# Index 5 of a fused attention and expert kernel takes index 6's order: a fourth group of seven products in place of four dense row blocks

## The chip, the cores and the metric

The kernel runs on one core of a Trainium2 chip. The metric is the time of one execution on the device in microseconds (us); of several executions the median is given. The core has five engines that work side by side and wait for each other through semaphores: TensorE (PE: matmuls; PEld: the loads of their stationary operands), VectorE (DVE), ScalarE (ACT), GpSimd (POOL) and SyncE (SP), which here issues nearly all transfers.

## The reference

Two steps. First, attention in chunks: `q`, `k` and `v` are (8 batches, 8 heads, 576 rows, 64), and each run of 64 rows attends to itself alone.

```python
scores = scale * np.matmul(q_c, k_c.transpose(0, 1, 2, 4, 3))
attn = np.exp(scores - np.max(scores, axis=-1, keepdims=True))
attn = attn / (np.sum(attn, axis=-1, keepdims=True) + 1e-09)
out = np.matmul(attn, v_c)
```

Then the heads are laid side by side, which gives `x` of 4608 tokens by 512, and a two-layer network with an exact Gelu follows:

```python
h = x @ w_in                                    # w_in 512 x 2048
g = 0.5 * h * (1.0 + erf(h * inv_sqrt2))
return (g @ w_out).astype(np.float32)           # w_out 2048 x 512
```

All inputs and the output are float32.

## The kernel before

The tokens are worked in nine tiles of 512 (`NT = 9`, index `t` from 0 to 8): tile `t` under 8 holds the first 512 rows of batch `t`, tile 8 the last 64 rows of all eight batches. All matmuls are in bfloat16 with sums in float32. One index runs in two halves.

First half, `mm1_seven` (from L599): h = Gelu(x w_in), held transposed in 16 row blocks of 128 features by 512 tokens. A row block can be computed dense, by `mm1_slot` (L450 to L457): four matmuls of 512 columns into one PSUM bank, then a Gelu of 128x512 on ScalarE (L457). Or four row blocks at once form a group, by `seven_rows` (L559): the group's 2 x 2 block product is made from seven block products in place of eight, in the manner of Strassen and Winograd. Each product is four matmuls of 256 columns (L574). It needs sums of blocks of x (`x_sums`, L557, on VectorE, once per tile) and of w_in (made once, early). The steps of a group are:

- `p1` to `p7`: the seven products, into three PSUM banks a, b and d; `p5` also copies its bank to a place in SBUF (`kept`, L586), `p3` ends with a Gelu;
- `s11`: ScalarE copies bank a into b (L587), so that p1 serves twice;
- `s12` and `c22+`: VectorE adds `kept` and bank a (L578);
- `c11`, `c12`, `c22`: Gelu of a finished block, on ScalarE (L582).

A step of group 0 stands without a mark, of group 1 with ', of group 2 with '' and of group 3 with '''. A number in an order (12 to 15) is a dense row block. Group g makes the row blocks 4g to 4g + 3.

Second half, `mm2_seven` (from L668): the output as seven products of its own, 16 matmuls of 256 columns each (L730). Two `Y` steps stand for one product. It needs sums of blocks of h (`S1a` to `S4b`, L653 and L666, VectorE), copies of its first results on ScalarE (L690) and additions on VectorE (L695), and then the stores.

Between these steps stands the attention for the tiles behind: `T0` (totals of the softmax of tile t + 1), `R0` to `R3` (their reciprocals spread out), `AV` (attn times v, TensorE), `X0` to `X3` (x), `XS1` to `XS4` (sums of blocks of x), `KC0` to `KC3` (k of tile t + 2 laid out by chunks, ScalarE), `S` (scores of tile t + 2, TensorE, and their Exp), `P0` to `P3` (partial sums of the softmax of tile t + 2, VectorE: L256 and L259), `exp` and `gelu` (a load of ScalarE's function table).

The order of the work on every engine is the order of the program: a manual schedule, in which each engine runs its own instructions in the order in which they were written, and waits where an operand or a buffer isn't ready. For the indices 4 to 8 that order is a list of steps written out by hand (`FOURTH`, `LATER`, `SIXTH`, `SEVENTH`, `LAST`); the table `WHOLE` (L492) says which index takes which list. The table `FURTHER` (L493) gives the groups 2 and 3 of an index their PSUM pools for the banks a, b and d. There are three pools: `MM` with three banks, `TP` with two, `AT` with three. A bank is taken again once its last reader is done. The place for `kept` of the groups 2 and 3 is an old arrival buffer of a load (`kept_home`, from index 4 on).

Indices 6, 7 and 8 have four groups, index 5 three groups and the dense row blocks 12 to 15.

Of the kernel before, what the change touches and what calls it, by code (L numbers as in the profile page):

```python
# [11 lines left out]
def kernel(  # L12
# [15 lines left out]
    B, H, S, D = q.shape  # L28
# [10 lines left out]
    NT = B + 1  # L39
# [176 lines left out]
    AT, TP, MM = (ps_at, "at"), (ps_tp, "tp"), (ps_mm, "mm")  # L216
# [159 lines left out]
    def att_sum_pe(t, g):  # L376

        pT = tiles[t]["pT", g]
        sT = ps_at.tile([P, MT // P, 2], f32, tag="at", name="sT")
        for m in range(MT // P):  # L380
            nc.tensor.matmul(sT[:, m], pT[:].rearrange("p i c -> p (i c)")[:, m * P:(m + 1) * P], ones_r[:],
                             start=True, stop=True)
        rr = work.tile([P, MT // P, 2], f32, tag="rr", name="rr", bufs=2)
        nc.vector.reciprocal(rr[:], sT[:])

        def spread():
            rc_ps = ps_mm.tile([P, MT], f32, tag="mm", name="rc_ps")
            for m in range(MT // P):
                for r in range(2):
                    nc.tensor.matmul(rc_ps[CH * r:CH * (r + 1), m * P:(m + 1) * P],  # L390
                                     rr[:, m, r:r + 1].to_broadcast([P, D]), ident_f[:],
                                     start=True, stop=True, tile_position=(0, CH * r))
            rc = work.tile([P, NB, 32], f32, tag="rc", name="rc", bufs=4)
            nc.scalar.copy(rc[:].rearrange("p n e -> p (n e)"), rc_ps[:])
            tiles[t]["rc", g] = rc
        return spread
# [53 lines left out]
    def mm1_slot(t, f):  # L450
# [3 lines left out]
        for ks in range(KS):  # L454
# [5 lines left out]
    T0 = 3  # L460
    DENSE = (0,)
    TWICE = tuple(range(2, NT))
    FOURTH = ("p1", "s11", 11, "p1'", "p2", "s11'", "c11", "p6", 9, "p5'", "p5", "p6'", 14, "s12'", "s12", "p2'", 13, 10, "p4'",
# [4 lines left out]
    LATER = ("p1", "s11", "p5", "p1'", "p1''", "p2", "p6", "c11", "s11'", "s11''", 13, "s12", 14, "p2''", "c11''", "p6'", "p4",  # L468
# [5 lines left out]
    SIXTH = ("p1", "s11", "p1''", "s11''", "p5", "p5''", "p2", "p6", "s12", "p6''", "p2''", "s12''", "p1'", "c11", "p7", "c11''",  # L474
# [12 lines left out]
    LAST = ("p1", "p1'", "s11", "p5", "p1'''", "s11'", "p2", "p6", "s12", "c11", "p2'", "p5'''", "p5'", "c11'", "s11'''", "p6'",  # L487
# [4 lines left out]
    WHOLE = {T0 + 1: FOURTH, T0 + 2: LATER, NT - 3: SIXTH, NT - 2: SEVENTH, NT - 1: LAST}  # L492
    FURTHER = {T0 + 2: ((MM, AT, AT),), NT - 3: ((MM, MM, MM), (MM, MM, AT)),  # L493
               NT - 2: ((MM, MM, MM), (MM, AT, MM)), NT - 1: ((MM, TP, AT), (MM, TP, MM))}

    HF = FF // 2
# [102 lines left out]
    def mm1_seven(t, hooks):  # L599
# [9 lines left out]
        if t in TWICE:  # L609
            does.update((step + "'", do) for step, do in  # L610
                        seven_rows(t, 1, {"a": TP, "b": TP, "d": AT}, kept[1], more).items())
            if t not in WHOLE:
                fifth = does["p5'"]
                does["p5'"] = lambda: (more.update(d=bank["b"]), fifth())
        for of, pools in enumerate(FURTHER.get(t, ()), 2):
            if kept_more:
# [3 lines left out]
            does.update((step + "'" * of, do) for step, do in seven_rows(t, of, dict(zip("abd", pools)), home, {}).items())  # L620
        if t in WHOLE:
            order = WHOLE[t][:WHOLE[t].index("Y0")]
        elif t == T0:
# [239 lines left out]
    def act_table(func):  # L863
        nc.scalar.activation(act_scratch[:], rest[:, 0:1], func)  # L864

    with tc.manual_schedule():
# [46 lines left out]
        p2 = att_sum_pe(0, 2)  # L913
        p3 = att_sum_pe(0, 3)
# [63 lines left out]
        def whole_hooks(t):  # L978

            n = t + 1  # L980
            acts = {f"S{i}{'ab'[a]}": lambda i=i, a=a: g_sum(t, i, a) for i in (1, 2, 4) for a in range(2)}
            acts["S3"] = lambda: g_sum(t, 3)
            if n < NT:
                acts.update(T0=lambda: quad_totals(n), AV=lambda: quad_av(n, ALONE),
                            exp=lambda: act_table(Act.Exp), gelu=lambda: act_table(Act.Gelu))
                for m in range(G):
                    acts[f"R{m}"] = lambda m=m: quad_rc(n, m // 2, m % 2)
                    acts[f"X{m}"] = lambda m=m: quad_x(n, m // 2, m % 2)
                    acts[f"XS{m + 1}"] = lambda m=m: x_sums(n, (m,))
            if n + 1 < NT:  # L990
                acts["S"] = lambda: quad_S(n + 1, ALONE)
                for m in range(G):
                    acts[f"KC{m}"] = lambda m=m: k_by_chunk(n + 1, AC, (m,))
                    acts[f"P{m}"] = lambda m=m: quad_part(n + 1, m // 2, m % 2)
            e1, e2, slot = {}, {}, 0
            for step in WHOLE[t]:
                if str(step)[0] == "Y":
                    slot += 1
                elif step in acts:
                    if slot:  # L1000
                        e2.setdefault(slot, []).append(acts[step])
                    else:
                        e1[step] = [acts[step]]
            if t + 4 == NT - 1:
                e2.setdefault(11, []).append(lambda: [load_qk(NT - 1, "q"), pool_cast_qk(NT - 1, "q")])
            return e1, e2
# [17 lines left out]
        for t in range(1, NT):  # L1024
# [40 lines left out]
            exp, gelu = lambda: act_table(Act.Exp), lambda: act_table(Act.Gelu)  # L1065
# [5 lines left out]
            if t <= T0:  # L1071
# [24 lines left out]
                else:  # L1096
# [3 lines left out]
                    e2[13] = parts[1]  # L1100
            if t in WHOLE:
                e1, e2 = whole_hooks(t)
# [29 lines left out]
```

## Time and profile before

| what | value |
| --- | --- |
| median of three runs | 268.07 us (267.96 to 268.8) |
| the profiled execution | 269.33 us, span 266.6 us |
| TensorE busy | 257.2 us, 96% of the span |
| VectorE busy | 226.9 us, 85% |
| ScalarE busy | 198.5 us, 74% |
| GpSimd busy | 89.9 us, 34% |
| index 5, from its first matmul to that of index 6 | 160.60 to 187.18 us |
| index 6, likewise | 187.18 to 213.13 us |

The span is the time from the first to the last instruction of the profiled execution; the time of the whole execution also holds what lies around it. Rows of the views name the line, the engine, the operation, and output and inputs by the program's tile names. A row of the timeline begins with start and length in us and puts neighbours of one kind together (x4); its brackets give the idle time before it and what ended it. Matmuls overlap one another, so a single one is listed as longer than the distance to the next. A line can be a helper's: L574 is every product of a group, L578 every addition of `s12` and `c22+`.

### The profile page before, as it was taken

What the parts mean: (1) busy time and instruction counts of PE and PEld (TensorE: products, weight loads), DVE (VectorE), ACT (ScalarE), POOL (GpSimd) and SP (SyncE); (2) the same over time, 40 slices, a digit from 0 to 9 for tenths busy, and PEclk for the clock granted to TensorE, in tenths of its full rate; (3) what the DMA queues carried; (4) which work ended last, traced back from release to release, by engine and by line L of the source; (5) the groups of instructions that cost most, each with busy time, mean ns of one, the idle gap of its engine ahead of it and who ended that gap; (6) DMA issues with size and microseconds to landing.
All of it is one profiled execution on the core that took longest, in us unless ns stands there. A gap on an engine that the chain in (4) does not pass through costs nothing.

```text
span 266.6 us, 7515 instructions
## 1 busy us (share of the span) xinstructions
PE 257.2 (96%) x3023; PEld 202.2 (76%) x3037; DVE 226.9 (85%) x379; ACT 198.5 (74%) x386; POOL 89.9 (34%) x142
## 2 busy tenths in 40 slices
PE   7699999999999999999999999999999999999994
PEld 2478775556886688668876887788888888888883
DVE  6874877999997998988999899897999999947853
ACT  3766758888676967889977987897799789227820
POOL 7869769431177211910710930305100300000000
PEclk9999999999999999999999999999999999999999
DMA  6999998899799899999889929999863320121014
GB/s 203 283 327 401 394 403 212 236 225 281 224 383 268 198 179 312 234 246 318 218 232 309 249 84 170 231 141 164 233 150 88 98 81 2 42 79 42 2 39 118
DMA packets 104739, 53.97 MB, mean 202 GB/s; under 512 B 72960, under 2 KB 101632, under 8 KB 104704
## 3 DMA queue, kind: packets, MB, share of 16 engines
q1 hardware_dynamic: 104400, 53.23, 76.2%
q8 instruction: 23, 0.38, 0.6%
q10 hardware_dynamic: 304, 0.26, 0.3%
q14 instruction: 12, 0.10, 0.1%
HBM read 36.70 MB, written 9.44 MB: 173 GB/s over the span
## 4 chain that ended last, share of the span: by engine, by line
PE 61%; DMA 15%; SPq 13%; ACT 4%; POOL 3%; DVE 2%; issue 1%; POOLq 0%
PE y_ps L730 30%; PE hs_ps L574 21%; DMA arrival<-in_moe_w_out_dram 8%; SPq L128 6%; PE h_ps L455 5%; SPq L194 4%; DMA arrival<-in_k_dram 3%; SPq L116 3%; DMA arrival<-in_v_dram 2%; DMA k_t<-k_nat 2%; PE av_ps L312 1%; ACT k_bd L188 1%; POOL w_out_sb L853 1%; SPq L118 1%; PE s_ps L239 1%
## 5 line engine op out<-in xcount | busy, mean ns | idle before, releaser
L582 ACT ACTIVATE h<-hs_ps 128x512 bf16<-128x512 f32 x66 | 37.7, 602 | 5.1 <-PE hs_ps L574 4.1
L730 PEld LDWEIGHTS <-h 128*128 128x128 bf16 x384 | 37.1, 98 | 4.9 <-issue 0.2
L164 POOL CAST q_nat<-arrival 128x512 bf16<-128x512 f32 x31 | 21.8, 742 | 53.2 <-DMA arrival<-in_q_dram 40.5
L457 ACT ACTIVATE h<-h_ps 128x512 bf16<-128x512 f32 x49 | 29.3, 601 | 11.6 <-PE h_ps L455 7.3
L455 PE MATMUL h_ps<-x,w_in_sb 128*128 128x512 bf16 x131 | 33.3, 379 | 0.5
L214 POOL CAST v_nat<-arrival 128x1024 bf16<-128x1024 f32 x14 | 15.9, 1143 | 44.3 <-DMA arrival<-in_v_dram 44.3
L730 PE MATMUL y_ps<-v_bd,k_bd 128*128 128x256 bf16 x256 | 29.8, 273 | 0.2
L730 PE MATMUL y_ps<-w_out_sb,h 128*128 128x256 bf16 x256 | 29.8, 273 | 0.0
L574 PEld LDWEIGHTS <-w_in_sb 128*128 128x128 bf16 x264 | 25.7, 98 | 4.6 <-issue 0.2
L730 PEld LDWEIGHTS <-k_bd 128*128 128x128 bf16 x256 | 24.8, 98 | 3.7 <-issue 0.5
L164 POOL CAST k_nat<-arrival 128x512 bf16<-128x512 f32 x30 | 20.5, 718 | 15.6 <-DMA arrival<-in_v_dram 12.0
L574 PE MATMUL hs_ps<-x,w_in_sb 128*128 128x256 bf16 x176 | 24.4, 273 | 0.0
L695 DVE TENSOR_TENSOR kept<-y_ps,kept 128x512 f32<-128x512 f32 (+1 forms) x25 | 16.4, 657 | 6.9 <-issue 4.2
L455 PEld LDWEIGHTS <-w_in_sb 128*128 128x128 bf16 x140 | 13.7, 98 | 11.0
L690 ACT COPY kept<-y_ps 128x512 f32<-128x512 f32 (+1 forms) x26 | 14.4, 558 | 9.7 <-PE y_ps L730 9.5
L864 ACT ACT_TABLE_LOAD x16 | 20.5, 1283 | 1.0 <-PEq L1116 0.7
L730 PE MATMUL y_ps<-v_bd,s_sb 128*128 128x256 bf16 x128 | 16.0, 273 | 0.0
L246 ACT ACTIVATE pT<-s_ps 128x512 bf16<-128x512 f32 x28 | 14.4, 599 | 1.5 <-PE s_ps L239 1.4
L730 PE MATMUL y_ps<-w_out_sb,s 128*128 128x256 bf16 x128 | 15.3, 273 | 0.0
L730 PE MATMUL y_ps<-v_bd,h 128*128 128x256 bf16 x128 | 15.3, 272 | 0.0
L574 PEld LDWEIGHTS <-w_in_more 128*128 128x128 bf16 x128 | 12.5, 98 | 3.6 <-issue 0.4
L429 PE MATMUL h_ps<-x,w_in_sb 128*128 128x256 bf16 x128 | 14.3, 273 | 0.0
(146 smaller groups left out, 558.3 us busy)
## 6 DMA issues: line engine op xcount, KB each, us to landing
arrival<-in_v_dram SPq DMA_DIRECT2D x58, 128.0 KB, 4.4
arrival<-in_q_dram SPq DMA_DIRECT2D x7, 1024.0 KB, 6.8
arrival<-in_k_dram SPq DMA_DIRECT2D x6, 1024.0 KB, 8.0
out_dram<-kept SPq DMA_DIRECT2D x21, 256.0 KB, 2.7
arrival<-in_moe_w_out_dram SPq DMA_DIRECT2D x4, 1024.0 KB, 11.6
arrival<-in_moe_w_in_dram SPq DMA_DIRECT2D x6, 512.0 KB, 7.7
out_dram<-y_sb SPq DMA_DIRECT2D x11, 256.0 KB, 3.0
arrival<-in_k_dram SPq DMA_DIRECT2D x8, 256.0 KB, 5.2
```

Of the source, the lines that this page charges most:

```text
L128: nc.sync.dma_start(to, rows.rearrange("h key d -> key h d"))
L164: copy(st[nm][:, g].rearrange("p j r d -> p r j d"), st[nm + "f"][:, 2 * g:2 * g + 2])
L214: copy(st["v"][:, r::2], st["vf"][:, r::2])
L246: nc.scalar.activation(pT[:].rearrange("p u (c j) -> p u c j", j=J), s_ps[g2][c][:].rearrange("p u (j c) -> p u c j", j=J), Act.Exp, scale ...
L455: (nc.tensor.matmul if t else by_halves)(h_ps[:], w_in_sb[:, ks, f * P:(f + 1) * P], tiles[t]["x"][:, ks, :], start=(ks == 0), stop=(ks == ...
L457: nc.scalar.activation(tiles[t]["h"][:, f, :], h_ps[:], Act.Gelu)
L574: nc.tensor.matmul(hs[:, f], left[:, ks, f * P:(f + 1) * P], right[:, ks], start=(fresh and f == 0 and ks == 0), stop=(ks == 1), skip_grou ...
L582: nc.scalar.activation(h[:, n:n + HM, HD * c:HD * (c + 1)], src, Act.Gelu)
L690: nc.scalar.copy(kept[name][:, ms], ps[:])
L695: nc.vector.tensor_tensor(y_sb[:, ms], ps[:], y_sb[:, ms], op=ADD)
L730: nc.tensor.matmul(to, left(f, m), right[:, f], start=(fresh and (split or m == 0) and f == 0), stop=(f == HF - 1), skip_group_check=True)
L864: nc.scalar.activation(act_scratch[:], rest[:, 0:1], func)
```

## The change

Index 5 drops its own list `LATER` and takes `SIXTH`, the list of index 6. In `SIXTH` the row blocks 12 to 15 are made by group 3 and not one by one. The table of pools changes with it: index 5's group 2 had (MM, AT, AT) and there was no group 3; now group 2 has (MM, MM, MM) and group 3 (MM, MM, AT), as in index 6.

```diff
-    LATER = ("p1", "s11", "p5", "p1'", "p1''", "p2", "p6", "c11", "s11'", "s11''", 13, "s12", 14, "p2''", "c11''", "p6'", "p4",
-             "T0", "c12", "p7", "p5'", "p2'", "p5''", "s12'", "c11'", "c22+", "p6''", 15, "s12''", "p7'", "c22", "c22+'", "p4'",
-             "c12'", "p3", "c22'", "p7''", "R2", "p3'", "c22+''", 12, "p4''", "c22''", "c12''", "p3''", "R3", "S3", "KC2", "S1b",
-             "S1a", "Y0", "Y0", "S2b", "S2a", "AV", "Y1", "KC0", "R1", "X3", "Y1", "X0", "Y2", "X2", "KC3", "exp", "X1", "Y2",
-             "KC1", "Y3", "Y3", "S4a", "Y4", "S4b", "XS1", "S", "XS3", "XS2", "Y4", "P0", "Y5", "gelu", "XS4", "P2", "Y5", "P1",
-             "Y6", "P3", "Y6")
     SIXTH = ("p1", "s11", "p1''", "s11''", "p5", "p5''", "p2", "p6", "s12", "p6''", "p2''", "s12''", "p1'", "c11", "p7", "c11''",
              "s11'", "p5'", "p4''", "p1'''", "p4", "c12''", "p6'", "c12", "T0", "s12'", "s11'''", "p2'", "p7''", "c11'", "p5'''",
              "p6'''", "p2'''", "p7'", "c22+", "c22", "c11'''", "c22+''", "c22''", "p4'", "c12'", "s12'''", "p3", "p7'''", "c22+'",
              "R1", "c22+'''", "p3'", "c22'", "R2", "S1a", "p4'''", "c12'''", "S3", "c22'''", "S1b", "p3''", "p3'''", "Y0", "KC0",
              "AV", "S2a", "Y0", "KC3", "KC2", "Y1", "S2b", "X2", "S4a", "X1", "X0", "R3", "X3", "KC1", "Y1", "Y2", "Y2", "S4b",
              "Y3", "XS1", "XS3", "exp", "Y3", "Y4", "S", "XS2", "Y4", "Y5", "P0", "gelu", "Y5", "Y6", "XS4", "P3", "P1", "P2",
              "Y6")
...
-    WHOLE = {T0 + 1: FOURTH, T0 + 2: LATER, NT - 3: SIXTH, NT - 2: SEVENTH, NT - 1: LAST}
-    FURTHER = {T0 + 2: ((MM, AT, AT),), NT - 3: ((MM, MM, MM), (MM, MM, AT)),
+    WHOLE = {T0 + 1: FOURTH, T0 + 2: SIXTH, NT - 3: SIXTH, NT - 2: SEVENTH, NT - 1: LAST}
+    FURTHER = {T0 + 2: ((MM, MM, MM), (MM, MM, AT)), NT - 3: ((MM, MM, MM), (MM, MM, AT)),
                NT - 2: ((MM, MM, MM), (MM, AT, MM)), NT - 1: ((MM, TP, AT), (MM, TP, MM))}
```

`T0` is 3 here and `NT` 9, so `T0 + 2` is index 5 and `NT - 3` index 6. The lists of the other indices stay, index 8's four groups among them. The unchanged list `SIXTH` is shown because it is what index 5 now runs. Line numbers after the removed list are smaller by six in the changed kernel.

## Prediction

> **What bounds the kernel now.** I read the page first: its busy row and its clock row.
>
> ```profile
> span 266.6 us, 7515 instructions
> PE 257.2 (96%) x3023; PEld 202.2 (76%) x3037; DVE 226.9 (85%) x379; ACT 198.5 (74%) x386; POOL 89.9 (34%) x142
> PEclk9999999999999999999999999999999999999999
> ```
>
> TensorE is busy for 96% of the span and the granted clock never falls. A share for the whole span says little about indices 5 and 6, so I next read the chain of work that ended last there, where the change lies.
>
> ```profile
> 160.76 2.62 PE hs_ps L574 x24
> 163.43 1.67 PE h_ps L455 x7
> ...
> 173.38 1.75 PE y_ps L730 x16
> 175.13 0.66 PE av_ps L312 x64
> ...
> 183.57 3.77 PE y_ps L730 x33
> 187.35 12.23 PE hs_ps L574 x112
> 199.57 0.87 PE y_ps L730 x8
> ```
>
> The chain is nothing but TensorE: no wait on VectorE, ScalarE or a transfer stands in either index. A TensorE instruction that is removed here shortens the span, as long as nobody is late for the one behind it. The third view is the table of windows, cut at the first matmul of each half (first half: tokens times w_in; second: the output products).
>
> ```profile
> 160.60:173.22 12.62, 12.52 (x100) 9.78 (x100) 11.65 (x24) 10.76 (x21) 2.29 (x4) 1.00 1.17 201
> 187.18:199.41 12.23, 12.23 (x114) 10.96 (x112) 11.96 (x25) 11.00 (x22) 1.04 (x1) 1.00 0.82 205
> 173.22:187.18 13.96, 13.91 (x242) 11.93 (x240) 12.20 (x22) 11.97 (x18) 3.52 (x5) 1.00 0.99 147
> 199.41:213.13 13.72, 13.72 (x243) 11.97 (x240) 13.48 (x22) 12.43 (x20) 2.30 (x2) 1.00 0.36 93
> ```
>
> Columns: window, its length, then busy time and count of PE, weight loads, DVE, ACT, POOL, the granted clock, the transfer engines' share, GB/s. The rows are index 5 first half, index 6 first half, index 5 second half, index 6 second half. Index 6 already runs the order that index 5 is to get, so its rows show what that order costs: 12.23 us against 12.62, with TensorE never idle but VectorE busy for 11.96 of 12.23. VectorE is the engine to watch.
>
> **The change part by part.** *The products.* Four dense blocks (4 x 4 matmuls of 512 columns) go, seven products (7 x 4 matmuls of 256) come.
>
> ```profile
> 168.44 1.03 PE L455 MATMUL h_ps<-x,w_in_sb 128*128 128x512 bf16 x4
> 169.30 0.60 PE L574 MATMUL hs_ps<-k_bd,w_in_more 128*128 128x256 bf16 x4
> 169.74 0.60 PE L574 MATMUL hs_ps<-x,w_in_more 128*128 128x256 bf16 x4
> ```
>
> Matmuls overlap, so their spacing counts and not their length: four dense ones take 169.30 - 168.44 = 0.86 us and four of a product 169.74 - 169.30 = 0.44. Out go 4 x 0.86 = 3.45 us, in come 7 x 0.437 = 3.06 (0.437 because index 6's 28 products take 12.23). Saved: 0.39 us, and the windows agree with 12.62 - 12.23 = 0.39. I take -0.39.
>
> TensorE: Matmul & The Clock Gate in the Trainium skill (Back-to-back issue gap) speaks against this exchange: it gives sustained spacings of about 81 ns at 128 columns and 131 at 512. An estimate between the two, some 98 ns at 256, would make the products 28 x 98 = 2.7 us against 16 x 131 = 2.1, a loss of 0.6 us. The rows above show 215 and 109 ns in this very stage, so the trace disagrees with that rule and agrees with the isolated gaps on the same page, which grow with the columns.
>
> *The work on ScalarE and VectorE.* The dense blocks had four evictions through Gelu, the group has four of the same size. New are two copies on ScalarE (s11''', p5''') and two additions on VectorE (s12''', c22+''').
>
> ```profile
> L587 ACT COPY hs_ps<-hs_ps 128x512 f32<-128x512 f32 x4 | 2.3, 582 | 0.0
> L578 DVE TENSOR_TENSOR hs_ps<-hs_ps,arrival 128x512 f32<-128x512 f32 x2 | 1.4, 690 | 0.0
> ```
>
> That is about 2 x 0.58 = 1.2 us more for ScalarE and 2 x 0.69 = 1.4 for VectorE (less where they overlap their neighbours). ScalarE goes from 10.76 to about 12 of 12.2 at the most, index 6 shows 11.00: covered. VectorE goes to what index 6 has, 11.96 of 12.23: covered only if it starts index 5 no later than it starts index 6. So I compared the starts.
>
> ```profile
> 163.26 0.69 DVE L259 TENSOR_REDUCE part<-pt 128x16 f32<-128x512 bf16 x1
> 163.86 0.69 DVE L578 TENSOR_TENSOR hs_ps<-hs_ps,kept_p 128x512 f32<-128x512 f32 x1
> ...
> 190.07 0.70 DVE L578 TENSOR_TENSOR hs_ps<-hs_ps,kept_p 128x512 f32<-128x512 f32 x1
> 190.68 0.69 DVE L578 TENSOR_TENSOR hs_ps<-hs_ps,arrival 128x512 f32<-128x512 f32 x1
> ...
> 196.59 0.68 DVE L578 TENSOR_TENSOR kept_p<-hs_ps,kept_p 128x512 f32<-128x512 f32 x1
> ...
> 197.87 0.69 DVE L578 TENSOR_TENSOR arrival<-hs_ps,arrival 128x512 f32<-128x512 f32 x1
> ```
>
> s12 starts 163.86 - 160.60 = 3.26 us into index 5 and 190.07 - 187.18 = 2.89 into index 6, both times straight behind the partial sums (L259) that the stage before left over. Index 5 is 0.37 us worse off, and that is unchanged by the edit. In the new order s12 is wanted early: p7 is the tenth product, and it adds to the bank that s12 reads.
>
> ```profile
> 187.18 1.04 PE L574 MATMUL hs_ps<-x,w_in_sb 128*128 128x256 bf16 x8
> ...
> 191.11 0.60 PE L574 MATMUL hs_ps<-k_bd,w_out_sb 128*128 128x256 bf16 x4
> ...
> 59.27 0.69 DVE L578 TENSOR_TENSOR hs_ps<-hs_ps,kept_p 128x512 f32<-128x512 f32 x1
> ...
> 60.01 0.60 PE L574 MATMUL hs_ps<-x,w_in_more 128*128 128x256 bf16 x4
> ```
>
> In index 6, p7 starts at 191.11, 3.93 after the first matmul, and s12 was over at 190.77: 0.34 to spare. In index 5, p7 would be due at 160.60 + 3.93 = 164.53, and s12 ends at 163.86 + 0.69 = 164.55; the last two rows show 0.05 us from such an addition's end to the matmul that waits for it. **So p7 gets a wait of about 0.07 us that index 6 does not have.** Behind it on TensorE stands the whole rest of the index. The later waits on VectorE, carried over from index 6 by the distance from s12 (nothing idles between): s12'' ends at 165.16, p4'' due at 160.60 + 11 x 0.437 = 165.41; c22+' ends 6.52 + 0.68 after s12's start, at 171.06, p3' due at 171.09; c22+''' ends 7.80 + 0.69 after it, at 172.35, p3''' due at 172.40. With the 0.05 they come out between early and 0.02 late, and TensorE has lost 0.07 by then. I take +0.07 in all; the ends are 0 (s12 a little quicker) and 0.4 (index 5's full handicap of 0.37 paid).
>
> *What moves.* SP and POOL have the same instructions in the same order in both programs, so no transfer is passed by another. Their rows matter in one place: p5'' is fourth in the new order, and ScalarE's copy of it goes into half of an old arrival buffer, so it waits for the cast that emptied it.
>
> ```profile
> 153.34 2.02 POOL L214 CAST v_nat<-arrival 128x1024 bf16<-128x1024 f32 x2
> 168.03 2.29 POOL L164 CAST q_nat<-arrival 128x512 bf16<-128x512 f32 x4 [12.66 <-DMA out_dram<-kept]
> 168.24 0.59 ACT L586 COPY arrival<-hs_ps 128x512 f32<-128x512 f32 x1 [0.33 <-PE hs_ps L574]
> ```
>
> Before, that copy ran at 168.24 while the first of the four casts begun at 168.03 was still going, so what it waits for on POOL had ended by 155.36. The new place, about 162.5, is safe: 0. Were it to wait after all, everything on ScalarE would stand behind it. The hooks of the second half (k_c copies, Exp table load, x) take index 6's places, and there nothing of them is on the chain: 0. The tightest by its rows is S2, which VectorE ends at 202.68 in index 6 for products that start at 203.65; 0.37 later is still early.
>
> ```profile
> 201.40 1.28 DVE L666 TENSOR_TENSOR k_bd<-k_bd,h 128x1024 bf16<-128x1024 bf16 x2
> 203.65 3.66 PE L730 MATMUL y_ps<-v_bd,k_bd 128*128 128x256 bf16 x32
> ```
>
> *One stray gap.* Index 5's second half is 13.96 - 13.72 = 0.24 longer than index 6's with the same matmuls. Nearly all of it is one late weight load.
>
> ```profile
> 183.57 0.10 PEld L730 LDWEIGHTS <-s_sb 128*128 128x128 bf16 x1 [0.32 <-issue]
> ```
>
> "issue" names no releaser; the other seven loads of that block had just run. Nothing in the edit explains why it should go, so it stays in the sum; -0.24 to 0 goes into the range.
>
> **The sum.** -0.39 + 0.07 = -0.32 us. The profiled execution took 269.33 us (span 266.6 and 2.7 around it) and becomes 269.0; it is 1.26 over the median of the three runs, 268.07, so the time I predict is 268.07 - 0.32 = 267.75, rounded to 267.7.
>
> **The rivals.** *A, VectorE falls behind into index 6 (slower).* The x sums (L557) now come at about 163.86 + (207.82 - 190.07) = 181.6 to 183, where POOL casts k.
>
> ```profile
> 181.54 0.76 DVE L557 TENSOR_TENSOR k_bd<-x 128x512 bf16<-128x512 bf16 x2
> 183.95 0.69 DVE L695 TENSOR_TENSOR kept<-y_ps,kept 128x512 f32<-128x512 f32 x1 [1.31 <-PE y_ps L730]
> 182.31 2.47 POOL L164 CAST k_nat<-arrival 128x512 bf16<-128x512 f32 x4 [11.99 <-DMA arrival<-in_v_dram]
> 207.49 2.30 POOL L214 CAST v_nat<-arrival 128x1024 bf16<-128x1024 f32 x2 [17.70 <-DMA arrival<-in_v_dram]
> 207.82 2.25 DVE L557 TENSOR_TENSOR k_bd<-x 128x512 bf16<-128x512 bf16 x2
> ```
>
> Beside a cast two of them took 2.25 us, alone 0.76. (GPSIMD Engine Reference in the Trainium skill, Specifications, says that POOL shares its SBUF interfaces with VectorE for instructions with two SBUF inputs; these rows agree.) That is up to 1.5 us more, against the 1.31 of idle time at 183.95, of which the two new additions leave little. If 0.8 comes through, s12 of index 6 ends 0.8 later, less its 0.34 to spare: p7 there waits 0.5, and the time is 267.75 + 0.5 = 268.25. It decides once more than 0.34 + 0.32 = 0.66 us of lateness reaches index 6. Against it: the partial sums behind wait for step 5 of the output in any case, and that hides the first part. *B, index 5 becomes index 6 entirely:* 12.23 + 13.72 for 12.62 + 13.96, -0.63: 267.45. For it: equal orders; against it: the 0.37. *C, 256 columns cost more than half of 512* in the longer run of products (weight loads no longer hidden under them): +0.6 by the same count, 268.7; the 28 x 4 back-to-back matmuls of index 6 at 109 ns speak against it.
>
> **How the numbers follow.** Forecast 0.63 (its own range 267.5 to 268.0), A 0.18, B 0.14, C 0.02, something unseen 0.03. The runs spread from 267.96 to 268.8, so a median may sit 0.1 lower or some tenths higher. The range 267.2 to 268.6 reaches over B and A with that. A measurement of this kernel can tell 0.3%, 0.8 us, from no change, and none of the cases reaches that by its own price. Slower 0.12: half of A (the lateness is handed on from index 6 to 7 and paid again), 0.01 of C and 0.02 of the unseen. Faster 0.06: 0.05 of B with a low draw of the runs, 0.01 unseen. Within 0.3%: the other 0.82.
>
> **What would show it.** In the profile after, no L455 rows in index 5; 28 groups of four hs_ps matmuls in 12.2 to 12.35 us; a gap of under 0.15 us at the tenth product, released by DVE; VectorE without idle time until the sums of h; index 6 at 25.95 or up to 0.2 more. Wrong: a hole ended by DVE or ACT of over 0.3 us in index 5, 6 or 7; L557 rows over 1 us near 182; or product spacing above 0.45 us per four.

## The result, and the profile after

The changed kernel takes 267.85 us (median of 22 runs, 267.4 to 269.55). The kernel before, run beside it on the same chip, takes 268.71 (22 runs, 267.6 to 271.29). The ratio is 0.9961, 95% interval 0.9942 to 0.9979: between 0.56 and 1.56 us less. The ratios, here and below, leave out the one run that was over 1.5% above its kernel's fastest, and are not the quotient of the two medians. The profiled execution took 267.66 us (269.33 before).

The page of the changed kernel, its busy row and two of its queues (packets, megabytes, share of 16 transfer engines):

```profile
span 265.9 us, 7563 instructions
PE 258.9 (97%) x3049; PEld 204.6 (77%) x3049; DVE 224.4 (84%) x381; ACT 199.0 (75%) x388; POOL 90.2 (34%) x142
...
q1 hardware_dynamic: 104400, 53.23, 73.9%
q8 instruction: 24, 0.39, 0.6%
```

The windows of the changed kernel, with the columns of the prediction's table: index 5 first half, index 5 second half, index 6 whole.

```profile
160.44:172.74 12.30, 12.30 (x114) 10.94 (x112) 12.00 (x26) 11.00 (x22) 2.29 (x4) 1.00 1.17 210
172.74:186.46 13.72, 13.72 (x242) 11.98 (x240) 13.08 (x23) 12.44 (x20) 3.71 (x5) 1.00 1.01 169
186.46:212.41 25.95, 25.95 (x354) 22.96 (x352) 24.89 (x46) 23.43 (x40) 3.57 (x3) 1.00 0.53 135
```

Index 5 fell from 12.62 + 13.96 to 12.30 + 13.72 us. The first half lost 0.32, the predicted sum exactly. The second half lost 0.24, which the prediction had kept. Index 6 is unchanged.

The chain of work that ended last in the changed kernel, through index 5:

```profile
160.61 12.30 PE hs_ps L568 x112
172.91 0.87 PE y_ps L724 x8
...
182.15 4.47 PE y_ps L724 x40
```

It is still TensorE alone. The block of the late weight load, in the changed kernel's timeline, has all eight loads in a row:

```profile
182.08 0.77 PEld L724 LDWEIGHTS <-s_sb 128*128 128x128 bf16 x8
```

The line numbers are 6 smaller, since the old list of names went. The predicted wait shows in the timelines of the changed kernel, TensorE's first (start, us, tile):

```profile
163.06 0.60 PE L568 MATMUL hs_ps<-k_bd,arrival 128*128 128x256 bf16 x4
163.50 1.04 PE L568 MATMUL hs_ps<-x,w_in_sb 128*128 128x256 bf16 x8
164.45 0.60 PE L568 MATMUL hs_ps<-k_bd,w_out_sb 128*128 128x256 bf16 x4
```

then VectorE's:

```profile
163.71 0.69 DVE L572 TENSOR_TENSOR hs_ps<-hs_ps,kept_p 128x512 f32<-128x512 f32 x1
...
181.35 0.76 DVE L551 TENSOR_TENSOR k_bd<-x 128x512 bf16<-128x512 bf16 x2
182.03 0.83 DVE L551 TENSOR_TENSOR k_bd<-x,k_bd 128x512 bf16<-128x512 bf16 x1
183.22 0.69 DVE L689 TENSOR_TENSOR kept<-y_ps,kept 128x512 f32<-128x512 f32 x1 [0.36 <-ACT pT L246]
```

Eight matmuls from 163.50 end their spacing at 163.50 + 8 x 0.109 = 164.37; p7 starts at 164.45. By the starts of the single matmuls the gap is 0.076 us. s12 runs from 163.71 to 164.40 and p7 starts 0.05 after it. Further down, two x sums together take 0.76 us, not the 2.25 of rival A. The third, beside POOL's cast of k, takes 0.83 us, twice the 0.41 of the next one at 185.52, and VectorE still has 0.36 us of idle time left before step 5 of the output.

Where the time went is read from the starts of the indices (first hs_ps or h_ps matmul of each) in three profiled executions of each program: the first pair, and two unchanged repeats of each that are described below. Each entry is a length in us, worked out from these starts:

```
                          idx0   idx1   idx3   idx5          idx6   idx0 to end
before                    32.40  28.42  28.06  12.62+13.96   25.94  248.96
before, second profile    32.38  28.17  28.06  12.62+13.75   25.96  248.52
before, third profile     32.54  28.23  28.06  12.62+14.08   25.94  249.16
changed                   32.22  28.17  28.22  12.30+13.72   25.95  248.14
changed, second profile   32.23  28.18  28.26  12.30+13.72   25.95  248.19
changed, third profile    32.22  28.17  28.06  12.30+13.72   25.95  248.00
mean difference           -0.22  -0.10  +0.12  -0.32 -0.21   0      -0.77
```

Two terms were not predicted: the second half of index 5, and indices 0 and 1, whose instructions the edit does not touch.

### The profile page after: what moved, and what is told of

It reads as the page before. It is cut to its first block, busy times and chain, and to the rows that moved or that the text cites. A ratio compares the mean times of both kernels' runs of the same rounds, so it can differ in the third digit from the quotient of the medians.

```text
span 265.9 us, 7563 instructions
## 1 busy us (share of the span) xinstructions
PE 258.9 (97%) x3049; PEld 204.6 (77%) x3049; DVE 224.4 (84%) x381; ACT 199.0 (75%) x388; POOL 90.2 (34%) x142
## 3 DMA queue, kind: packets, MB, share of 16 engines
q1 hardware_dynamic: 104400, 53.23, 73.9%
## 4 chain that ended last, share of the span: by engine, by line
PE 87%; ACT 9%; DMA 1%; issue 1%; POOL 0%; SPq 0%; DVE 0%; POOLq 0%
PE y_ps L724 33%; PE hs_ps L568 26%; PE h_ps L455 9%; PE h_ps L429 5%; PE y_ps L794 3%; ACT pT L246 2%; PE av_ps L312 2%; PE h_ps L445 2%; ACT L858 1%; ACT h L457 1%; PE tp L175 1%; PE y_ps L758 1%; DMA arrival<-in_k_dram 1%; ACT k_bd L188 1%; ACT h L576 1%; PE s_ps L239 1%
## 5 line engine op out<-in xcount | busy, mean ns | idle before, releaser
L576 ACT ACTIVATE h<-hs_ps 128x512 bf16<-128x512 f32 x69 | 39.4, 602 | 4.9 <-PE hs_ps L568 4.0
L457 ACT ACTIVATE h<-h_ps 128x512 bf16<-128x512 f32 x45 | 26.9, 602 | 11.1 <-PE h_ps L455 7.1
L214 POOL CAST v_nat<-arrival 128x1024 bf16<-128x1024 f32 x14 | 16.7, 1196 | 42.6 <-DMA arrival<-in_v_dram 41.9
L455 PE MATMUL h_ps<-x,w_in_sb 128*128 128x512 bf16 x124 | 30.7, 379 | 0.0
L568 PEld LDWEIGHTS <-w_in_sb 128*128 128x128 bf16 x276 | 26.9, 98 | 4.5 <-issue 0.2
L164 POOL CAST k_nat<-arrival 128x512 bf16<-128x512 f32 x30 | 19.7, 692 | 17.8 <-DMA arrival<-in_v_dram 11.8
L568 PE MATMUL hs_ps<-x,w_in_sb 128*128 128x256 bf16 x184 | 25.6, 273 | 0.0
```

Of the source, the lines that this page charges most:

```text
L164: copy(st[nm][:, g].rearrange("p j r d -> p r j d"), st[nm + "f"][:, 2 * g:2 * g + 2])
L214: copy(st["v"][:, r::2], st["vf"][:, r::2])
L455: (nc.tensor.matmul if t else by_halves)(h_ps[:], w_in_sb[:, ks, f * P:(f + 1) * P], tiles[t]["x"][:, ks, :], start=(ks == 0), stop=(ks == ...
L457: nc.scalar.activation(tiles[t]["h"][:, f, :], h_ps[:], Act.Gelu)
L568: nc.tensor.matmul(hs[:, f], left[:, ks, f * P:(f + 1) * P], right[:, ks], start=(fresh and f == 0 and ks == 0), stop=(ks == 1), skip_grou ...
L576: nc.scalar.activation(h[:, n:n + HM, HD * c:HD * (c + 1)], src, Act.Gelu)
```

## The experiments

The theory: the products save 0.39, p7 gives back as much as s12 is late, and nothing is handed on. The rivals: VectorE hands its lateness to index 6 (A); index 5 becomes index 6 entirely, stall included (B). A third question came with the result: is the gain larger than the trace explains?

**Both kernels again.** No edit; each program ran in two more sessions.

> The kernel before, unchanged, timed against itself. Theory 1 (the 0.24 us in index 5's second half was a stray stall of one execution): ratio 1 within its interval, and in this profile the second half of index 5 lasts 13.72 us, without a gap at the last matmul of the m = 1 block behind the scores. Theory 2 (the stall belongs to the list LATER and comes in every execution): 13.9 us or more again, gap of 0.2 us at the same matmul. The spread of the single times tells how far a difference of 0.3% is to be trusted.

> The changed kernel again. Theory 1 (only the products and the new wait): index 5 takes 26.0 us in the profile, first half 12.30 with a gap of 0.07 to 0.08 us at the tenth product, and the time is 0.3 to 0.6 us under that of the kernel before (ratio 0.9978 to 0.9989). Theory 2 (the change also takes stalls away that the traces of one execution do not show): ratio near the 0.9961 of the result, under 0.997.

> The kernel before against itself once more, to see how far the times of one program scatter. Theory 1 (the rest of the difference between the medians is scatter ahead of index 4): in the profile index 4 to the end takes 132.6 us again, what varies lies ahead of it; fastest span 265.4 to 265.9 us. Theory 2 (the program before has stalls in index 4 and behind that the changed one lacks): a look with index 4 to the end over 132.8 us.

> The changed kernel once more, beside the kernel before on the same chip. Theory 1: index 5 26.02 us and index 4 to the end 132.2 us again; the medians of spans are 0.3 to 0.5 us under those of before, if the scatter hits both alike. Theory 2: 0.7 us or more under before for the third time, which no row of index 5 explains.

Measured against the kernel before of the same session: before again 268.81 (ratio 0.9991, 0.9966 to 1.0017) and 268.75 (0.9986, 0.9958 to 1.0015); changed again 268.00 (0.9966, 0.9942 to 0.9990) and 267.97 (0.9963, 0.9938 to 0.9987). The gain of about 0.35% is there in all three sessions. In index 5 the changed kernel does what the first theory expected (26.02 us, with a gap of 0.079 and 0.080 at p7); the time does what the second expected, a ratio under 0.997, where the products and the wait alone would give 0.9978 to 0.9989.

Windows of index 5's second half, the kernel before in its second profile:

```profile
172.62:186.37 13.75, 13.75 (x242) 11.94 (x240) 12.20 (x22) 12.06 (x18) 3.42 (x5) 1.00 1.03 162
```

and in its third, with the weight load from its timeline:

```profile
173.34:187.42 14.08, 13.92 (x243) 11.94 (x241) 13.05 (x23) 11.98 (x18) 3.72 (x5) 1.00 1.02 160
```

```profile
182.70 0.66 PEld L730 LDWEIGHTS <-s_sb 128*128 128x128 bf16 x7
183.79 0.10 PEld L730 LDWEIGHTS <-s_sb 128*128 128x128 bf16 x1 [0.44 <-issue]
```

and the changed kernel in its third profile:

```profile
161.50:173.80 12.30, 12.30 (x114) 10.95 (x112) 12.00 (x26) 10.99 (x22) 2.29 (x4) 1.00 1.17 196
173.80:187.52 13.72, 13.72 (x242) 12.01 (x240) 12.66 (x23) 12.45 (x20) 3.28 (x5) 1.00 1.01 165
```

The late load is not a stray of one execution: it sits at the same eighth load of the same block in two of three profiles of the kernel before, and in none of the changed one. From index 4 to the end the kernel before takes 132.58 us without it (second profile) and 133.00 with it (third), the changed one 132.20 to 132.22. The first half is the same to 0.01 us in all profiles of each program.

**One half of the order at a time.** First, index 5 gets the new first half and keeps the old order of the second (R1 and R3 as before, KC2 ahead of Y0):

```diff
-    WHOLE = {T0 + 1: FOURTH, T0 + 2: SIXTH, ...}
+    FIFTH = ("p1", "s11", "p1''", "s11''", "p5", "p5''", ..., "p3''", "p3'''", "KC2", "Y0",
+             "Y0", "S2b", "S2a", "AV", "Y1", "KC0", "R3", "X3", ..., "P3", "Y6")
+    WHOLE = {T0 + 1: FOURTH, T0 + 2: FIFTH, ...}
```

> Index 5 takes the first half of SIXTH (four groups) and keeps the second half of LATER with its places for the hooks (R3 where R1 was, k_c's first copy ahead of Y0). Theory 1 (the products carry the gain): first half 12.30 us, the 0.07 to 0.08 us wait at the tenth product included; second half 13.7 to 13.96; all of the gain but the stray gap, 0.3 us or more under before. Theory 2 (the order of the hooks carries it): second half at least 0.2 us longer than the 13.72 of the changed kernel, time within 0.15 us of before.

Measured 268.92 (ratio 0.9998, 0.9972 to 1.0024). Windows of index 5 of this kernel:

```profile
161.88:174.18 12.30, 12.30 (x115) 10.94 (x113) 12.00 (x26) 11.00 (x22) 2.29 (x4) 1.00 1.21 198
174.18:187.92 13.74, 13.74 (x242) 12.02 (x240) 13.15 (x22) 12.45 (x20) 3.55 (x5) 1.00 0.97 171
```

By the trace it is the changed kernel plus 0.02 us, and from index 4 to the end it takes 132.23 us against 132.20. So the forecast part of the gain belongs to the first half of index 5; the reordered second half is worth 0.02 to 0.03 us. There is no late load here either, with the old order of the second half, in this one profile. The runs do not show what the trace shows: the expected 0.3 us, a ratio of 0.9989, lies inside the interval, but the ratio is 0.003 above that of the changed kernel in the same session, for traces that differ by 0.03 us, or 0.0001. Either a single ratio is good to about 0.003 only, or this kernel stalls in executions that were not profiled; no run tells which. The gain of the products is therefore shown by the traces and not by this kernel's times.

Second, the other way round: three groups and the dense blocks, then index 6's second half.

```diff
-    WHOLE = {T0 + 1: FOURTH, T0 + 2: SIXTH, ...}
-    FURTHER = {T0 + 2: ((MM, MM, MM), (MM, MM, AT)), ...}
+    FIFTH = ("p1", "s11", "p5", "p1'", ..., 13, "s12", 14, ..., "p3''", "R1", "S3", "S1b", "S1a",
+             "Y0", "KC0", "AV", "S2a", ..., "P2", "Y6")
+    WHOLE = {T0 + 1: FOURTH, T0 + 2: FIFTH, ...}
+    FURTHER = {T0 + 2: ((MM, AT, AT),), ...}
```

> Index 5 keeps three groups and the dense row blocks 12 to 15 in the order of LATER, and takes the second half of SIXTH alone. Theory 1: first half 12.62 us as before, with no wait at p7; second half 13.72; time as before or up to 0.25 us less. Theory 2 (the order of the hooks carries the gain): time 0.5 us or more under before.

Measured 269.55 (ratio 1.0004, 0.9973 to 1.0035). Windows of index 5 of this kernel:

```profile
162.37:174.99 12.62, 12.62 (x102) 9.79 (x100) 11.74 (x24) 10.76 (x21) 2.29 (x4) 1.00 1.17 183
174.99:188.71 13.72, 13.72 (x242) 11.99 (x240) 12.35 (x22) 11.99 (x18) 3.27 (x5) 1.00 1.06 172
```

The dense first half costs its 12.62 again, and the second half ran without the late load. In this profile index 4 takes 0.6 and the last index 1.8 us more than in the others, so only its indices 0 and 5 are read. Since the kernel before also has one profile without the late load, this single one does not tell whether the new second half removes it.

**p7 one product later.** This takes away the wait by giving s12 more time:

```diff
-    ... "p1'", "c11", "p7", "c11''", "s11'", "p5'", "p4''", ...
+    ... "p1'", "c11", "c11''", "s11'", "p5'", "p7", "p4''", ...
```

It stands in index 5's list alone. It ran in two sessions.

> The changed kernel with p7 of index 5 moved behind p5', so that it is the eleventh product's place less one later and due 0.44 us later than before. Theory 1 (p7 waits 0.08 us only because s12 is late by index 5's start): the gap goes, first half 12.23 us as in index 6, index 5 25.95. Rival (the lateness only moves to the next product that needs VectorE): a gap of 0.05 to 0.08 us stays at p3' or p3'''. The times of whole executions cannot tell 0.08 us.

> p7 one product later, beside the other two on the same chip. Theory 1: index 5 25.95 to 25.98 us, index 4 to the end 132.14, the median within 0.2 us of the changed kernel's. Theory 2 (the 0.9927 of its first run was real): 0.7 us or more under the changed kernel.

Measured 268.04 (ratio 0.9927, 0.9906 to 0.9948) and 268.27 (0.9976, 0.9947 to 1.0005). Window of index 5's first half, the first session:

```profile
161.16:173.41 12.25, 12.25 (x115) 10.94 (x113) 11.95 (x26) 11.00 (x22) 2.30 (x4) 1.00 1.15 204
```

The wait at p7 is gone; a gap of 0.029 us is left before p3', which adds to the bank that c22+' reads: the one later wait that the prediction had put at up to 0.02. So the first half reaches 12.25, 0.05 better, and not the 12.23 of the first theory. In the second session it is 12.25 again, with a gap of 0.023, and index 5 takes 25.96 us; there index 4 took 26.99 in place of 26.77, for a reason that stays open. In time this kernel cannot be told from the changed one: the second session has it 0.30 us above the changed kernel, and in the first the changed kernel did not run beside it. The ratio of 0.9927 did not come again, and the kernel is not shown to beat the changed one.

**One more sum ahead of s12.** A tensor_reduce that nobody uses makes VectorE late by a known amount. In both kernels the edit reaches index 5 only, although the first expectation also speaks of index 6.

```diff
+    more_sum = consts.tile([P, 16], f32, name="more_sum")
...
+            acts["D"] = lambda: nc.vector.tensor_reduce(
+                more_sum[:], rest[:].rearrange("p (n e) -> p n e", e=32), axis=mybir.AxisListType.X, op=ADD)
...
-    ... "p2", "p6", "s12", "p6''", ...
+    ... "p2", "p6", "D", "s12", "p6''", ...
```

> The changed kernel with one more sum on VectorE (128x16 out of 128x512, the size of L259, result unused) in front of s12 in index 5 and index 6. Theory 1 (index 5 has no slack left on VectorE at p7, index 6 has 0.34 us less the release): p7 waits 0.08 + 0.60 = 0.68 us in index 5 (first half 12.90) and, since VectorE is free for 0.2 us ahead of s12 in index 6, about 0.1 us there (12.33); nothing else moves. Rival (VectorE has slack that takes it up, or the lateness grows from index to index): first half of index 5 under 12.6, or index 6 and 7 longer by 0.3 or more.

> The kernel with one more sum on VectorE ahead of s12 again, since in its first run VectorE came 0.9 us late out of index 4. Theory 1 (p7 pays VectorE's lateness one for one, nothing is handed on): first half of index 5 12.30 + 0.60 = 12.90 us if index 4 is 26.77, more by as much as s12 starts later; index 6 25.95 to 26.05. Rival: index 6 or 7 longer by 0.3 or more.

Measured 274.26 us (one run; before of that session 269.84) and 272.15 (one run; before 268.62). VectorE's and TensorE's timelines, the second of the two runs (L575 and L579 here are L574 and L578 of the kernel before):

```profile
166.95 0.69 DVE L259 TENSOR_REDUCE part<-pt 128x16 f32<-128x512 bf16 x1
167.55 0.68 DVE L985 TENSOR_REDUCE more_sum<-rest 128x16 f32<-128x512 bf16 x1
168.14 0.69 DVE L579 TENSOR_TENSOR hs_ps<-hs_ps,kept_p 128x512 f32<-128x512 f32 x1
```

```profile
166.98 1.04 PE L575 MATMUL hs_ps<-x,w_in_sb 128*128 128x256 bf16 x8
168.89 0.60 PE L575 MATMUL hs_ps<-k_bd,w_out_sb 128*128 128x256 bf16 x4 [0.87 <-DVE hs_ps L579]
```

and the same spot in the first:

```profile
170.20 0.69 DVE L579 TENSOR_TENSOR hs_ps<-hs_ps,kept_p 128x512 f32<-128x512 f32 x1
```

```profile
168.48 1.04 PE L575 MATMUL hs_ps<-x,w_in_sb 128*128 128x256 bf16 x8
170.94 0.60 PE L575 MATMUL hs_ps<-k_bd,w_out_sb 128*128 128x256 bf16 x4 [1.42 <-DVE hs_ps L579]
```

Counted from index 5's first matmul, s12 starts 3.26 us in for the changed kernel, 4.22 in the second of these and 4.78 in the first (0.60 of it the sum, the rest work that VectorE brought late out of index 4). The gap at p7, by the spacing of the matmuls ahead, is 0.076, 1.04 and 1.59 us. So s12 is 0.956 and 1.512 later, and p7 waits 0.96 and 1.51 more: **one for one**. The first halves are 13.26 and 13.81 us, 0.36 and 0.91 over the 12.90 expected, by as much as s12 came later than the sum alone makes it. Index 5's second half stays 13.72 and index 6 25.97 and 25.95. In these two kernels even 1.5 us of lateness in index 5 reaches nothing behind it.

Index 5 accounts for 1.5 us in the first run and 1.0 in the second; the rest of these times arises ahead of it and is described in the last section.

**Index 6 with the dense blocks.** The old exchange, one index later; index 5 stays changed.

```diff
-    WHOLE = {..., NT - 3: SIXTH, ...}
-    FURTHER = {..., NT - 3: ((MM, MM, MM), (MM, MM, AT)), ...}
+    WHOLE = {..., NT - 3: LATER, ...}
+    FURTHER = {..., NT - 3: ((MM, AT, AT),), ...}
```

> The changed kernel with the opposite edit in index 6: it takes the old list LATER with the dense row blocks 12 to 15 and three groups. Theory 1 (a group is worth 0.39 us of TensorE in whichever index): first half of index 6 12.62 us instead of 12.23, second half 13.72, index 5 unchanged at 26.02. Rival (the value depends on the index or on the list): a difference under 0.3 or over 0.5 us, or waits.

Measured 269.84 us, one run. Windows of index 6 of this kernel:

```profile
187.15:199.78 12.63, 12.53 (x101) 9.79 (x101) 11.38 (x23) 10.76 (x21) 1.79 (x2) 1.00 0.81 201
199.78:213.52 13.74, 13.74 (x242) 12.01 (x240) 13.03 (x23) 11.97 (x18) 2.33 (x2) 1.00 0.39 102
```

12.63 for 12.23: the group is worth the same 0.40 there, and the second half has no late load in this one profile.

**Three groups and a dense rest in index 4.** VectorE is given more to do one index earlier, where in the changed kernel it is already busy for 25.65 of 26.76 us: index 4 gets index 5's old list.

```diff
-    WHOLE = {T0 + 1: FOURTH, T0 + 2: SIXTH, ...}
+    WHOLE = {T0 + 1: LATER, T0 + 2: SIXTH, ...}
-    FURTHER = {T0 + 2: ..., ...}
+    FURTHER = {T0 + 1: ((MM, AT, AT),), T0 + 2: ..., ...}
```

> The change carried on: on top of it index 4 takes the list LATER, three groups and four dense row blocks in place of two groups and eight. Theory 1 (the gain needs VectorE's cover): VectorE is busy for 25.65 of index 4's 26.76 us, 1.2 to 1.4 us of additions come, 26.9 to 27.1 against the 26.37 that TensorE would need; so VectorE sets the length, waits appear in index 4 or at p7 in index 5, and the sum of both indices is no shorter than now (52.78 us). Rival (only TensorE counts): index 4 falls to 26.37 us and the time by another 0.39 us.

Measured 269.71 (ratio 1.0012, 0.9984 to 1.0040). Index 4's two windows:

```profile
133.66:148.28 14.62, 12.81 (x100) 9.68 (x100) 14.25 (x30) 11.14 (x23) 3.38 (x6) 1.00 1.02 288
148.28:162.59 14.31, 13.92 (x242) 11.95 (x240) 13.84 (x23) 12.09 (x18) 6.64 (x6) 1.00 0.41 105
```

and the wait in TensorE's timeline:

```profile
140.81 0.60 PE L574 MATMUL hs_ps<-x,w_out_sb 128*128 128x256 bf16 x4 [1.71 <-DVE hs_ps L578]
```

VectorE is busy for 14.25 + 13.84 = 28.1 of index 4's 28.9 us, and TensorE stands 1.7 us at the first product that needs s12. The index grows from 26.76 to 28.94, while the profit of a group is 0.4. So VectorE becomes the bound, as the first theory said, but the index is 1.8 us longer than the 26.9 to 27.1 that it expected; why is open. In the changed kernel's index 5 VectorE is busy for 12.00 + 13.08 of 26.02 us, and TensorE waits 0.08.

The same kernel shows rival A's path. In the second half of its index 5 an x sum meets a cast on POOL (POOL's timeline, then VectorE's):

```profile
187.43 1.04 POOL L214 CAST v_nat<-arrival 128x1024 bf16<-128x1024 f32 x1
187.60 1.15 DVE L557 TENSOR_TENSOR k_bd<-x,k_bd 128x512 bf16<-128x512 bf16 x1
```

The sum takes 1.15 us instead of 0.41. In index 6 s12 then starts 3.35 us in, and not 2.89, and p7 waits 0.16 us by the spacing; index 6 takes 26.10 us instead of 25.95. Lateness can be handed on, then; in the changed kernel it was not.

## Why the prediction was right or wrong

**The products, -0.39: right.** 12.62 became 12.30 with the wait and 12.25 almost without it; less the gap of 0.029 that is 12.22, against 12.23 in index 6. The counter-experiment in index 6 gives 0.40.

**The wait of p7, +0.07: right.** 0.076, 0.079 and 0.080 us in the three profiles, at the tenth product, with s12's end 0.05 us ahead of it. The sum ahead of s12 shows the mechanism: p7 pays VectorE's lateness one for one. The "end of 0.4" was too cautious: the comparison with index 6 leaves out the 0.34 us that index 6 had to spare.

**The new copies and additions hide behind TensorE: right.** ScalarE is busy for 11.00 of 12.30 us, VectorE for 12.00. With the new order in index 5, the only other wait in its first half is the 0.029 us before p3', where the prediction had "between early and 0.02 late".

**p5'', the hooks, POOL's and SP's order at 0: right.** p5'' causes no gap in the first half, and the products-only kernel shows the second half's order to be worth 0.02 us.

**Rival A: it did not come in the changed kernel.** Two x sums took 0.76 us near 181.4, the VectorE idle time before step 5 stayed open, and 1.5 us of lateness put in on purpose ended at p7. Its path exists all the same: in the kernel with three groups in index 4, an x sum of 1.15 us beside a cast made p7 of index 6 wait 0.16 us. **Rival C: refuted** by the spacing, 0.44 us per four throughout.

**Rival B, index 5 becoming index 6 entirely: nearly what came**, though for a reason it did not give. The wait of 0.076 is there, as forecast, and the late load is not.

**What failed: the step "One stray gap", and in it the sentence "Nothing in the edit explains why it should go, so it stays in the sum".** The second half is 0.24, 0.03 and 0.36 us over 13.72 in the three profiles of the kernel before, and 0 in each of three of the changed one. Of this 0.03 belongs to the old order without any late load (13.75 in the second profile, 13.74 in the products-only kernel), so the late load costs about 0.22, 0 and 0.33. As a mean the second half gives 0.21 us which the sum did not have. With the first half's 0.32, index 5 gives 0.53. The word "stray" was drawn from one profile. Neither "it stays" nor "it goes" could be read from it: the gap comes in some executions of one program and in none seen of the other.

A cause can be argued, though no run tested it. The gap has no releaser ("issue"). The page has a queue named "instruction" with pieces of 16 KB; its 24 pieces come to about 64 bytes for each of TensorE's 3049 matmuls and 3049 weight loads, so it seems to bring TensorE's program. The packet of this stage lands at these times (us from index 5's start; read from the single packets in the trace):

```
                      packet takes  lands at  eighth load runs at
before                1.68          21.70     22.97
before, second        1.71          21.36     22.74
before, third         1.12          21.82     23.08
```

By the spacing of the loads, the eighth was due at 22.66. In the two profiles with a gap it runs 1.27 us after the packet has landed; in the second profile 21.36 + 1.27 = 22.63 lies just ahead of the 22.66, and the load ran 0.08 late, which cost TensorE nothing. Such packets take 0.88 us at the least in these profiles, and more here. The transfer queues of the kernel before in the window from 180.4 to 182.4 us:

```profile
q1 hardware_dynamic: 1293, 0.33, 121.5%
```

(It is the time of the packets that start in the window, so it can pass 100%.) Against some 76% over the whole span that is a crowded stretch. In the changed program the packet starts 16.3 to 17.3 us into index 5. In its three profiles and in the eight of the other kernels it lands 17.1 to 20.2 us in, 2.4 us or more ahead of the eighth load, and none of them shows the gap. Why it comes earlier is open: the number of instructions is not the reason, for the kernel with only the second half changed has as many matmuls as the kernel before, and its packet lands at 18.6. All this fits, but no run moved the packet alone.

**Also unforeseen: indices 0 and 1 are together 0.32 us shorter in the mean**, though their code is the same. Index 0 is shorter in all three profiles of the changed kernel (32.22 or 32.23 against 32.38 to 32.54), index 1 only against two of the three before (28.17 or 28.18 against 28.42, 28.17 and 28.23). Index 0 takes 32.22 in the kernel with only the second half changed, too, and 32.23 in the one with dense blocks in index 6, which has as many matmuls as the kernel before; so the products are not what does it. The share of the transfer queue was 73.9 to 75.2% in the changed kernel's profiles and 75.9 to 76.2% in those of the kernel before, but the products-only kernel had 75.8% and still 32.22 for index 0. The cause is open.

So the traces show -0.77 us from index 0 on, of which -0.32 was predicted and has a shown cause. Ahead of index 0 the profiles scatter more than that: it begins 17.3 to 17.8 us into the span in the kernel before and 17.7 to 19.0 in the changed one, so that the whole spans of the two sets of three differ by 0.1 us only. The runs say -0.91 to -1.05 us (ratios 0.9961 to 0.9966). Their spans alone, in the mean of the second and the third session, are 266.23 and 266.24 us for the changed kernel and 266.92 and 266.88 for the kernel before: -0.69 and -0.64, and the rest lies outside the span. The runs' intervals hold the -0.77 as well as these; that of the first session begins at -0.56 and so leaves out the forecast -0.32 alone. That 267.7 comes within 0.15 us of 267.85 is partly luck: the sum started at 268.07, the median of three runs, while the kernel before, run beside the changed one, had 268.71. From there the forecast change gives 268.39. The chance of 0.06 for a gain of over 0.3% was too low for the same reason as the sum.

## What to carry to other kernels

When an index takes over a neighbour's order, compare when the covering engine starts in each: the difference, less the neighbour's slack at its first wait and plus the release (here 0.37 - 0.34 + 0.05 us), is the price, and further lateness is paid one for one. Price an exchange of matmuls by their spacing in that stage, not by the length of one. Before a gap without a releaser is called stray and kept in a sum, take a second and third profile of the same kernel: here the gap came at the same instruction in two of three, and in no profile of the other program.

## What the runs showed of the hardware that was not expected

**Stages that never touch it were longer in the two runs with one more tile of 64 bytes per partition.** Both kernels with the extra sum have it, allocated early. Their indices 0, 2 and 3, all ahead of the only instruction that writes it, take 1.4 to 1.6, 0.7 to 1.3 and 0.7 to 0.9 us more than the changed kernel's, and the transfers are the same in number and bytes. The row of the transfer queue, in the second kernel with the extra sum:

```profile
q1 hardware_dynamic: 104400, 53.23, 82.7%
```

in the first:

```profile
q1 hardware_dynamic: 104400, 53.23, 80.1%
```

and in the changed kernel of the second one's session:

```profile
q1 hardware_dynamic: 104400, 53.23, 74.6%
```

The same packets occupy the engines longer; one of 256 bytes takes 22.5 and 23.4 ns on average in these two runs, against 19.0 to 20.9 in the twelve others, where the queue's share is 73.9 to 76.8%. A shift of the later tiles' addresses by 64 bytes may be the cause, but that is only argued: the trace does not show addresses and no run varied them alone. The Trainium skill says in DMA: Bandwidth & Descriptors (How a descriptor splits into AXI transactions) that a descriptor which doesn't start on a 256-byte boundary needs an AXI transaction that also fetches the unused bytes before its start; the longer packets agree with it in direction. A constant added for an experiment can so cost more than what the experiment measures: here 0.96 and 1.51 us of the wait stand beside 3 us and more elsewhere.

**The busiest engine stood still at one fixed place without any semaphore**, by 0.22 and 0.33 us in two of three profiles; whether the late packet of instructions is the cause stays open, as said above.
